# Issuing operand sums three products ahead, and holding two older products back, in a fused attention and squared-ReLU MLP kernel

## The chip, the cores and the metric

The kernel runs on one core of one Trainium2 chip. The metric is device time in microseconds (us). Unless said otherwise, a quoted time is the median over the timed runs of a kernel.

The names of the engines are those of the profile: PE is the tensor engine's matmuls, PEld its weight loads, DVE the vector engine, ACT the scalar engine, POOL the GpSimd engine, SP the engine that issues most DMAs.

## The reference

```python
# attention, per batch (8) and head (12), S = 448, D = 64
scores = (1/sqrt(D)) * q @ k.T
attn   = maximum(scores, 0)**2 / S
x      = attn @ v                       # regrouped to 3584 tokens x 768
# MLP, w_in 768 x 2048, w_out 2048 x 768
h = x @ w_in
g = maximum(h, 0)**2
out = g @ w_out
```

## The kernel before

Attention for batch b+1 is woven into the MLP of batch b. A queue (`fifo`) holds the MLP's pieces, and each turn of the attention loop takes a share of it.

- "scores" (tile sp) are turned into tile at, by ACT and DVE or by ACT and POOL.
- "h groups" are x @ w_in: six matmuls each, then ACT and DVE make a slice of g from them.
- The last product, g @ w_out, is done for two 128-token chunks at once in Strassen-like form: seven products m1 to m7 of 8 matmuls each instead of eight. It needs four sums of blocks of g, made by DVE (tile comb):

```python
def s1(): combine("s1", nc.vector.tensor_add, get2()[:, lo], get2()[:, hi])
def s2(): combine("s2", nc.vector.tensor_sub, st["s1"], get1()[:, lo])
def s3(): combine("s3", nc.vector.tensor_sub, get1()[:, lo], get2()[:, lo])
def s4(): combine("s4", nc.vector.tensor_sub, get1()[:, hi], st["s2"])
# order of the products:      m1   m2   m6   m5   m7   m3   m4
# sums that must be made:      0    0    2    2    3    4    4
```

m1 and m2 read g directly. m6 reads s2, m5 reads s1, m7 reads s3 and m3 reads s4. Most products end in a "part" (ACT) or a "close" (DVE, tile osb) that takes the result out of PSUM.

This is where a sum is issued. All sums of a batch wait in a queue; a product takes from it what it needs, at the moment when it is itself issued:

```python
def item(k=k, fn=fn, need=due + (0, 0, 2, 2, 3, 4, 4)[k]):
    nonlocal used
    while made < need:
        sum_one()
    fn()
    used += 2 <= k < 6
```

The attention loop also issues one sum each turn, ahead of the two at operations, as long as fewer than six are unused (there are six buffers). Where several products are issued in one turn of the loop, or where the loop is over (the last batch), no such sum has been made, and the product itself issues it.

The work for batch b is queued by `push_dense(b)`. Products left over from earlier batches (`old`, from `backlog`) are spread between the 16 h groups:

```python
for i, g in enumerate(hs):
    push([g])
    upto = (i + 1) * len(old) // len(hs)
    for z in old[done:upto]:
        push(z)
    done = upto
...                     # rest copies of odd batches (POOL), then the new sums become available
for z in backlog[:now]: # new products: m1, m2, m6, ...
    push(z)
```

"rest" is a copy by POOL that gathers the last 64 tokens of two batches into one chunk.

Of the kernel before, what the change touches and what calls it, by code (L numbers as in the profile page):

```python
# [16 lines left out]
def kernel(  # L17
# [123 lines left out]
    def combine_w2(k, eng):  # L141
        a, step = k % 2, k // 2
        top, bot, r = w2[a], w2[2 + a], slice(4 * a, 4 * a + 4)
        if step == 0:
            eng.tensor_sub(t1[:, r], top[:, :, HI], top[:, :, LO])
        elif step == 1:
            eng.tensor_sub(t2[:, r], bot[:, :, HI], t1[:, r])
        elif step == 2:
            eng.tensor_sub(t4[:, r], t2[:, r], bot[:, :, LO])
        else:  # L150
            eng.tensor_sub(top[:, :, HI], bot[:, :, HI], top[:, :, HI])  # L151
# [10 lines left out]
    def push(work):  # L162
        nonlocal queued
        for c, fn in work:
            fifo.append((c, fn))
            queued += c
# [3 lines left out]
    def run_some(ns):  # L170
        nonlocal queued, credit
        credit += ns
        while fifo and credit > 0:
            c, fn = fifo.popleft()
            fn()
            queued -= c
            credit -= c
# [12 lines left out]
    def h_groups(b):  # L190
        gt = gts[b] = g_p.tile([P, NF, S], FP16, name="g", tag="g")
        xt = xts[b]

        def group(f):
            def run():
                hps = mm_p.tile([P, 512], FP32, name="hps", tag="mm")
                for m in range(NM):
                    nc.tensor.matmul(  # L198
                        hps[:, 0:S],
                        lhsT=w1[f // 4][:, m, (f % 4) * P:(f % 4 + 1) * P],  # L200
                        rhs=xt[:, m, :], start=(m == 0), stop=(m == NM - 1))
                relu2(hps[:, 0:S], gt[:, f, :], 1.0)
            return run

        return [(189.0 * NM, group(f)) for f in range(NF)]
# [10 lines left out]
    def rest(pr):  # L216
        t = rest_p.tile([P, NF, P], FP16, name="rest", tag="rest")
        for i in range(2):
            nc.gpsimd.tensor_copy(  # L219
                t[:, :, 64 * i:64 * i + 64], gts[2 * pr + i][:, :, 3 * P:S])  # L220
        rests[pr] = t

    def chunk(b, c):
        return lambda: gts[b][:, :, c * P:(c + 1) * P], [(b, 2 * c), (b, 2 * c + 1)]

    def rest_chunk(pr):
        return lambda: rests[pr], [(2 * pr, TJ - 1), (2 * pr + 1, TJ - 1)]

    def plain_groups(one):
        get, at = one  # L230

        def group(cols):
            def run():
                ps = mm_p.tile([P, 512], FP32, name="ops", tag="mm")
                for f in range(NF):
                    nc.tensor.matmul(  # L236
                        ps[:, 0:HALF], lhsT=get()[:, f, :], rhs=w2[f // 4][:, f % 4, cols],
                        start=(f == 0), stop=(f == NF - 1))
                osb = part_p.tile([P, HALF], FP32, name="osb", tag="part")
                nc.scalar.activation(out=osb, in_=ps[:, 0:HALF], func=AF.Copy, scale=CO)  # L240
                store(at, cols, osb)
            return run

        return [(162.5 * NF, group(cols)) for cols in (LO, HI)]
# [75 lines left out]
    sums: deque = deque()  # L320
    made = used = due = 0

    def sum_one():
        nonlocal made
        sums.popleft()()
        made += 1

    def chain(pairs):

        nonlocal due  # L330
        new = []
        for _, groups in pairs:
            for k, (c, fn) in enumerate(groups):
                def item(k=k, fn=fn, need=due + (0, 0, 2, 2, 3, 4, 4)[k]):
                    nonlocal used
                    while made < need:
                        sum_one()
                    fn()
                    used += 2 <= k < 6
                new.append([(c, item)])  # L340
            due += 4
        return new, lambda: sums.extend(fn for four, _ in pairs for fn in four)
# [4 lines left out]
    def push_dense(b):  # L347

        hs = h_groups(b)
        ready = None  # L350
        if b == 0:
            new = [[g] for c in range(2) for g in plain_groups(chunk(b, c))]
        elif b % 2 == 0:
            new, ready = chain([o_groups(chunk(b, 0), chunk(b, 1))])
        else:
            pr = b // 2
            pairs = [o_groups(chunk(b - 1, 2), chunk(b, 0)), o_groups(chunk(b, 1), chunk(b, 2))]
            if pr % 2 == 1:
                pairs.insert(1, o_groups(rest_chunk(pr - 1), rest_chunk(pr)))
            new, ready = chain(pairs)  # L360
        old = backlog[:QUOTA[b]]
        done = 0
        for i, g in enumerate(hs):
            push([g])
            upto = (i + 1) * len(old) // len(hs)
            for z in old[done:upto]:
                push(z)
            done = upto
            if b == 0 and 4 <= i < 16 and i % 2 == 1:
                push([(0.0, lambda k=(i - 4) // 2: combine_w2(k, nc.gpsimd))])  # L370
        if b % 2 == 1:
            push([(0.0, lambda: rest(b // 2))])
        if ready:
            push([(0.0, ready)])
        backlog[:] = backlog[len(old):] + new
        now = QUOTA[b] - len(old)
        for z in backlog[:now]:
            push(z)
        del backlog[:now]
        if b == 0:  # L380
            push([(0.0, lambda k=k: combine_w2(k, nc.gpsimd)) for k in (6, 7)])
# [7 lines left out]
    def scores(n, t):  # L389
        qT, kT = qkt[n, "q"], qkt[n, "k"]  # L390
        sp = s_p.tile([P, 2, 512], FP32, name="sp", tag="s")
        for e in range(2):
            for f in range(2):
                c = f ^ e
                r = slice(64 * f, 64 * f + 64)
                nc.tensor.matmul(  # L396
                    sp[64 * c:64 * c + 64, e, 0:S].rearrange("p (t c) -> p t c", t=TJ),
                    lhsT=kT[r, t, 64 * e:64 * e + 64],
                    rhs=qT[r, :, 64 * e:64 * e + 64], start=True, stop=True)
        return sp  # L400

    def soft(n, t, sp, pool=False):
        at = at_p.tile([P, 2, S], FP16, name="at", tag="at")
        if pool:
            relu2_wide(sp[:, :, 0:S], at, SK, nc.gpsimd)
        elif n < NU and t % 2 == 1:
            relu2_wide(sp[:, :, 0:S], at, SK, nc.gpsimd if n == 1 and t == 3 else nc.vector)
        else:
            relu2(sp[:, :, 0:S], at, SK)
        ats[n, t] = at  # L410
# [42 lines left out]
    def av_burst(n):  # L453
        return (TJ * (n + 1) - 1) // 2 + 2
# [25 lines left out]
    with tc.manual_schedule():  # L480
# [19 lines left out]
        for w in "kq":  # L500
# [3 lines left out]
        beside = {  # L504
            1: [(load_w1, 1)],
            2: [(cast_qk, 2, "k", pool), (cast_qk, 2, "q", pool),
                (load_qk, 3, "k", nc.sync), (load_qk, 3, "q", nc.sync)],
            3: [(turn_pe, 1, "k", dve), (load_w1, 2)],
            5: [(turn_pe, 1, "q", act), (load_w1, 3)],
            7: [(turn_pe, 2, "k", dve)],  # L510
            8: [(turn_pe, 2, "q", act), (load_v, 3)],
            9: [(cast_qk, 3, "k", pool), (cast_qk, 3, "q", pool),
# [11 lines left out]
        for r in range(STREAM):  # L524
# [5 lines left out]
            for fn, *a in beside.get(r, ()):  # L530
                fn(*a)
    tc.no_sync_barrier()
    push_dense(0)

    for i in range(STREAM // 2, NB):
        g = []
        for r in range(max(STREAM, 2 * i), 2 * i + 2):
            n, t = divmod(r, TJ)
            g.append((n, t, scores(n, t)))
        if sums and made - used < 6:  # L540
            sum_one()
        for z, a in enumerate(g):
            soft(*a, pool=z == 1 and (i > av_burst(2 * NU - 1) or i % 2 == 1))
        if i in avs:
            for t in range(TJ):
                av(avs[i], t)
        if i in pushes:
            push_dense(pushes[i])
        upkeep(i)
        nxt = min([j for j in pushes if j > i] or [NB + 2])  # L550
        run_some(max(0.0, (queued - KEEP) / (nxt - i)))
# [4 lines left out]
    for j in sorted(j for j in pushes if j >= NB):  # L556
        push_dense(pushes[j])
# [31 lines left out]
```

## Time and profile before

| | before |
|---|---|
| time, median of 2 runs | 465.34 us (463.84 to 466.84) |
| span of the profiled run | 464.5 us |
| PE busy | 396.0 us, 85% |
| PE idle (span less busy) | 68.5 us |
| of it, waiting for sums | 47.4 us in 19 waits |
| mean granted tensor engine clock | 0.937 |

The page gives the busy time of each engine, with its share of the span and the number of instructions. Of the second part of the page, the two rows below show PE's busy share and the granted clock in 40 slices of 11.6 us, in tenths (9 is 90% or more).

```profile
PE 396.0 (85%) x3000; PEld 194.2 (42%) x3000; DVE 283.0 (61%) x363; ACT 250.1 (54%) x386; POOL 223.4 (48%) x191
PE   6769998999599996997798998989479997896864
PEclk9756999999889998999889999999789999999899
```

PE bounds the kernel. After the start (the first five slices) its holes have a pattern: slices of 4 to 7 busy, and in or just behind most of them slices of clock below 9.

The list of waits names who waited for whom, with total us, number of waits and the longest.

```profile
PE ops L272 <- DVE comb L253: 47.4, 19, 6.0
PE sp L396 <- ACT rel L187: 6.6, 7, 1.6
PE sp L396 <- DVE at L181: 5.7, 8, 1.6
```

So the sums account for 47.4 of the 68.5 idle us. The timeline of the tail (batch 7, when no attention is left) shows how one such wait comes about. Columns: start in us, duration, engine, line, operation, what is written and read, number of instructions, and in brackets the idle time before it and what ended it. Rows that do not matter are cut.

```profile
418.35 2.76 PE L272 MATMUL ops<-w,g 128*128 128x384 f16 x16
...
421.20 0.56 DVE L283 SCALAR_TENSOR_TENSOR osb<-ops,part 128x384 f32<-128x384 f32 x1 [1.46 <-PE ops L272]
421.68 0.68 DVE L253 TENSOR_TENSOR comb<-g 128x1024 f16<-128x1024 f16 x1
422.39 0.69 DVE L253 TENSOR_TENSOR comb<-comb,g 128x1024 f16<-128x1024 f16 x1
...
423.14 2.77 PE L272 MATMUL ops<-wt,comb 128*128 128x384 f16 x16 [2.03 <-DVE comb L253]
...
427.78 0.56 DVE L283 SCALAR_TENSOR_TENSOR osb<-ops,part 128x384 f32<-128x384 f32 x1 [4.09 <-ACT part L278]
428.25 0.68 DVE L253 TENSOR_TENSOR comb<-g,comb 128x1024 f16<-128x1024 f16 x1
...
428.99 1.47 PE L272 MATMUL ops<-w,comb 128*128 128x384 f16 x8 [1.77 <-DVE comb L253]
```

The inputs of s1 and s2 were complete when the last g was written at 419.74. DVE had nothing to do from then to 421.20. But the close of m2 stands ahead of the sums in DVE's queue, and it can start only when PE has finished m2. So PE finishes m2, DVE closes it, DVE makes s1 and s2, and only then can PE go on with m6: 2.03 us. The same happens with s4, behind the close of m7, which itself starts only when ACT's part of m7 is done (the bracket): 1.77 us.

Beside attention the waits are longer, because a sum also meets POOL. This is batch 5, from the timeline of the kernel before:

```profile
328.90 0.96 POOL L96 CAST qs<-qf 128x896 f16<-128x896 f32 x1
328.96 5.06 DVE L253 TENSOR_TENSOR comb<-comb,g 128x1024 f16<-128x1024 f16 x1
329.78 2.04 POOL L219 COPY rest<-g 128x1024 f16<-128x1024 f16 x2
331.77 1.69 POOL L188 TENSOR_TENSOR at<-rel 128x896 f16<-128x896 f32 x1
```

And from its timeline of PE alone, the product that waited for the sum:

```profile
334.07 4.46 PE L272 MATMUL ops<-wt,comb 128*128 128x384 f16 x16 [6.05 <-DVE comb L253]
```

A sum of 0.68 us lasts 5.06 us, to 0.56 us after the end of POOL's unbroken run at 333.46. That POOL's run holds the sum is my reading of these times. The last line also shows the second cost: 16 matmuls in 4.46 us behind the wait, which take 2.77 us elsewhere. The granted clock was 0.50 from 331.5 to 337 us; the texts below call this half-rate.

### The profile page before, as it was taken

What the parts mean: (1) busy time and instruction counts of PE and PEld (TensorE: products, weight loads), DVE (VectorE), ACT (ScalarE), POOL (GpSimd) and SP (SyncE); (2) the same over time, 40 slices, a digit from 0 to 9 for tenths busy, and PEclk for the clock granted to TensorE, in tenths of its full rate; (3) what the DMA queues carried; (4) which work ended last, traced back from release to release, by engine and by line L of the source; (5) the groups of instructions that cost most, each with busy time, mean ns of one, the idle gap of its engine ahead of it and who ended that gap; (6) DMA issues with size and microseconds to landing.
All of it is one profiled execution on the core that took longest, in us unless ns stands there. A gap on an engine that the chain in (4) does not pass through costs nothing.

```text
span 464.5 us, 7617 instructions
## 1 busy us (share of the span) xinstructions
PE 396.0 (85%) x3000; PEld 194.2 (42%) x3000; DVE 283.0 (61%) x363; ACT 250.1 (54%) x386; POOL 223.4 (48%) x191
## 2 busy tenths in 40 slices
PE   6769998999599996997798998989479997896864
PEld 2434444444244443443344454444235443453432
DVE  3886885466756764667657766656846663454341
ACT  3876786566337763676256664757145772242101
POOL 6553799697526762566444654653724332000000
PEclk9756999999889998999889999999789999999899
DMA  9999992746637364563627355454513011200222
GB/s 257 290 259 216 243 191 51 180 120 138 139 87 148 69 155 116 87 159 102 155 53 174 66 147 157 71 137 117 95 35 73 1 35 34 52 0 19 67 68 51
DMA packets 67618, 53.57 MB, mean 115 GB/s; under 512 B 36864, under 2 KB 67584, under 8 KB 67584
## 3 DMA queue, kind: packets, MB, share of 16 engines
q1 hardware_dynamic: 55152, 40.84, 33.8%
q0 software_dynamic: 12160, 11.80, 16.2%
q8 instruction: 23, 0.38, 0.4%
q10 hardware_dynamic: 272, 0.46, 0.3%
q14 instruction: 11, 0.09, 0.1%
HBM read 45.61 MB, written 11.01 MB: 122 GB/s over the span
## 4 chain that ended last, share of the span: by engine, by line
PE 69%; DVE 11%; ACT 8%; issue 5%; POOL 4%; DMA 1%; SPq 1%; ACTq 0%; DVEq 0%; POOLq 0%
PE hps L198 27%; PE ops L272 25%; PE sp L396 7%; PE avt L428 6%; DVE comb L253 5%; DVE at L181 3%; ACT at L180 3%; ACT rel L187 2%; ACT part L278 1%; DVE osb L283 1%; PE ops L236 1%; PE warm L495 1%; POOL w L151 1%; POOL at L188 1%; DMA qf<-in_q_dram 1%
## 5 line engine op out<-in xcount | busy, mean ns | idle before, releaser
L188 POOL TENSOR_TENSOR at<-rel 128x896 f16<-128x896 f32 x67 | 112.4, 1678 | 148.1 <-ACT rel L187 148.0
L198 PE MATMUL hps<-xt,w 128*128 128x448 f16 x768 | 157.4, 356 | 1.1 <-ACT xt L435 0.7
L181 DVE SCALAR_TENSOR_TENSOR at<-sp,at 128x896 f16<-128x896 f32 x93 | 100.5, 1089 | 49.8 <-ACT at L180 49.3
L181 DVE SCALAR_TENSOR_TENSOR g<-hps,g 128x448 f16<-128x448 f32 x128 | 79.1, 623 | 57.8 <-ACT g L180 57.7
L198 PEld LDWEIGHTS <-w 128*128 128x128 f16 x768 | 72.5, 98 | 78.0 <-issue 17.2
L180 ACT ACTIVATE g<-hps 128x448 f16<-128x448 f32 x128 | 70.0, 549 | 62.8 <-PE hps L198 62.8
L180 ACT ACTIVATE at<-sp 128x896 f16<-128x896 f32 x93 | 84.1, 915 | 32.5 <-PE sp L396 32.4
L272 PEld LDWEIGHTS <-comb 128*128 128x128 f16 x416 | 40.8, 104 | 88.0 <-DVE comb L253 55.3
L278 ACT ACTIVATE part<-ops 128x384 f32<-128x384 f32 x52 | 25.6, 493 | 89.9 <-PE ops L272 89.8
L187 ACT ACTIVATE rel<-sp 128x896 f32<-128x896 f32 x75 | 69.3, 924 | 5.1 <-POOL at L188 2.9
L272 PE MATMUL ops<-wt,comb 128*128 128x384 f16 x208 | 44.7, 376 | 28.1 <-DVE comb L253 28.1
L396 PE MATMUL sp<-qT,kT 64*64 64x448 f16 x672 | 56.0, 391 | 13.4 <-ACT rel L187 6.6
L283 DVE SCALAR_TENSOR_TENSOR osb<-ops,part 128x384 f32<-128x384 f32 x52 | 28.8, 555 | 57.4 <-PE ops L272 29.6
L272 PE MATMUL ops<-w,comb 128*128 128x384 f16 x208 | 38.5, 329 | 19.4 <-DVE comb L253 19.4
L428 PE MATMUL avt<-at,vs 64*64 64x448 f16 x672 | 44.8, 379 | 0.9 <-DVE g L181 0.6
L396 PEld LDWEIGHTS <-kT 64*64 64x64 f16 x672 | 16.8, 109 | 47.1 <-issue 44.5
L272 PEld LDWEIGHTS <-g 128*128 128x128 f16 x264 | 25.7, 100 | 21.5 <-issue 6.2
L121 POOL DMA_DIRECT2D vs<-in_v_dram x48 | 29.9, 631 | 9.2 <-DMA w<-in_moe_w_in_dram 9.1
L272 PE MATMUL ops<-w,g 128*128 128x384 f16 x176 | 30.9, 326 | 0.0
L428 PEld LDWEIGHTS <-vs 64*64 64x64 f16 x672 | 22.4, 114 | 13.3 <-issue 3.4
L219 POOL COPY rest<-g 128x1024 f16<-128x1024 f16 x8 | 8.1, 1040 | 33.8 <-DVE g L181 33.8
L253 DVE TENSOR_TENSOR comb<-g 128x1024 f16<-128x1024 f16 x22 | 22.2, 1009 | 0.0
(45 smaller groups left out, 232.4 us busy)
## 6 DMA issues: line engine op xcount, KB each, us to landing
out_dram<-osb SPq DMA_DIRECT2D x112, 96.0 KB, 2.2
kf<-in_k_dram SPq DMA_DIRECT2D x22, 448.0 KB, 4.5
qf<-in_q_dram SPq DMA_DIRECT2D x21, 448.0 KB, 5.3
vs<-in_v_dram POOLq DMA_DIRECT2D x48, 112.0 KB, 4.1
w<-in_moe_w_in_dram POOLq DMA_DIRECT2D x4, 768.0 KB, 20.3
w<-in_moe_w_out_dram POOLq DMA_DIRECT2D x4, 768.0 KB, 18.7
early<-in_k_dram SPq DMA_DIRECT2D x2, 448.0 KB, 7.4
early<-in_q_dram SPq DMA_DIRECT2D x2, 448.0 KB, 9.2
```

Of the source, the lines that this page charges most:

```text
L121: nc.gpsimd.dma_start(out=t[64 * r:64 * r + 64], in_=src[:, u, hs])
L180: nc.scalar.activation(out=dst, in_=ps, func=AF.Square, scale=scale)
L181: nc.vector.scalar_tensor_tensor(out=dst, in0=ps, scalar=0.0, in1=dst, op0=ALU.is_gt, op1=ALU.mult)
L187: nc.scalar.activation(out=r, in_=ps, func=AF.Relu, scale=scale)
L188: eng.tensor_mul(dst, r, r)
L198: nc.tensor.matmul(hps[:, 0:S], lhsT=w1[f // 4][:, m, (f % 4) * P:(f % 4 + 1) * P], rhs=xt[:, m, :], start=(m == 0), stop=(m == NM - 1))
L253: op(t, x, y)
L272: nc.tensor.matmul(st[bank][:, 0:HALF], lhsT=st[a][:, j, :], rhs=w(j), start=(first and j == 0), stop=(j == NH - 1), skip_group_check=True)
L278: nc.scalar.activation(out=st[name], in_=st[bank][:, 0:HALF], func=AF.Copy, scale=CO)
L283: nc.vector.scalar_tensor_tensor(out=osb, in0=st[bank][:, 0:HALF], scalar=sign * CO, in1=st[name], op0=ALU.mult, op1=ALU.add)
L396: nc.tensor.matmul(sp[64 * c:64 * c + 64, e, 0:S].rearrange("p (t c) -> p t c", t=TJ), lhsT=kT[r, t, 64 * e:64 * e + 64], rhs=qT[r, :, 64 ...
L428: nc.tensor.matmul(ap[f][64 * e:64 * e + 64, 0:S], lhsT=vs[r, e ^ c, t * D:(t + 1) * D], rhs=at[r, e, :], start=(t == 0), stop=(t == TJ - ...
```

## The change

Intent: a product asks for the sums of the product three places further on (never past the end of its own batch's list, and never with six sums unused), so that they are in DVE's queue ahead of the closes that wait for PE. And two of the older products are kept out of the h groups and put behind them, so that PE has work while DVE makes the first sums of the new batch.

```diff
+    AHEAD, SUMS = 3, 6
...
+        last = due + 4 * len(pairs)
+        needs = (0, 0, 2, 2, 3, 4, 4)
         for _, groups in pairs:
             for k, (c, fn) in enumerate(groups):
-                def item(k=k, fn=fn, need=due + (0, 0, 2, 2, 3, 4, 4)[k]):
+                z = k + AHEAD
+                def item(k=k, fn=fn, need=due + needs[k],
+                         want=min(last, due + needs[z % 7] + z // 7 * 4)):
                     nonlocal used
-                    while made < need:
+                    while made < need or (made < want and made - used < SUMS):
                         sum_one()
...
         old = backlog[:QUOTA[b]]
+        beside = max(0, len(old) - 2)
...
-            upto = (i + 1) * len(old) // len(hs)
+            upto = (i + 1) * beside // len(hs)
...
         if ready:
             push([(0.0, ready)])
+        for z in old[done:]:
+            push(z)
```

No matmul, sum or transfer is added or removed. Batches 1, 3 and 7 have no older products, so for them only the first part acts.

More of the change, by code (lines that the diff above doesn't have):

```diff
@@ L539 @@
             g.append((n, t, scores(n, t)))
-        if sums and made - used < 6:
+        if sums and made - used < SUMS:
             sum_one()
```

## The prediction

> **What bounds the kernel now.** TensorE. The page's busy table: PE 396.0 of 464.5 us (85%), DVE 283.0, ACT 250.1, POOL 223.4; the chain that ended last is 69% PE and 5.3% sums (DVE "comb", L253). PE's largest idle item in the list of waits is PE ops L272 <- DVE comb L253: 47.4 us in 19 waits, longest 6.0. The PE timeline places them: batch 1, 3.95+2.60; batch 2, 3.95+1.77; batch 3, 3.95+2.60+1.39; batch 4, 2.03; batch 5, 6.05+2.60; batch 6, 2.03+1.32+1.77; batch 7 (tail, no attention left), three times 2.03+1.77 = 11.4.
>
> Issue order makes them: a sum enters DVE's queue only when its product is next, behind the close of the product before (which waits for PE) and behind "at" (1.09 us). A free sum takes 0.68 us, but the 52 take 55.9 us instead of 35.4: some last 2.07, 3.08 and 5.06 us, until a run of POOL ops ends. [...]
>
> The waits also cost clock: after them 16 matmuls take 4.45 us instead of 2.77. I count 13 us (3.0, 1.7, 3.3, 3.4, 1.7 at 120, 177, 222, 334, 436). [...] the granted clock there is 0.7 to 0.8.
>
> **What changes.** No matmul, sum or byte is added. s1 and s2 are issued before m1 (2.6 us of PE work cover 1.4 us of sums), s3 before m2, s4 before m6. In batches 2, 4, 5 and 6 two older products go behind the h groups: 2.6 us more cover. Batch 5's s2 would start about 2 us earlier, before POOL's run of casts.
>
> **Sum.** Tail: waits (11.4) and clock (1.7) go nearly whole: 21 products x 1.30 = 27.3 us plus the last 4.5, so 46 becomes 32 to 33. Batches 1 to 6: of 36 us of waits about 30 go; in batches 1 and 3 the "rest" copies (2 x 1.03 us on POOL, right behind h) still block s1, about 1 us each, and other collisions leave some 4. Clock: 9 of the remaining 11. Returned: "at" stands behind up to four sums (2.7 us), so scores and attention products wait longer, and new waits on ACT and POOL appear: 5 us. Net 13 + 30 + 9 - 5 = 47, rounded to 45: 465 becomes 420 us. Nearly all is on the critical path: PE had work behind every one of these waits.
>
> **Predicted: 420 us**, 8 in 10 between 410 and 434. Faster by over 2%: 0.95; within 2%: 0.04; slower: 0.01.
>
> **Signs.** Right: PE <- comb falls from 47.4 to under 10 us, none in the tail; PE busy about 385 us, over 90% of the span; no half-rate matmuls behind h; mean granted clock from 0.937 to about 0.96; tail after the last h 32 to 33 us; scores' waits for "at" and "rel" rise from 12 to at most 18 us. Wrong: sums last 2 us and more beside POOL and the comb waits stay, or scores, attention or h wait as much as was saved.
>
> **What would make it wrong.** Earlier sums may meet POOL's ops head on and hold DVE's queue, delaying "at" and g; a sum waiting for one of six buffers would block DVE; the half-rate clock may come back elsewhere.

## The result and the profile after

The changed kernel takes 415.38 us (414.22 to 416.55, 2 runs) against 465.34 us. The ratio is 0.8926, 95% interval 0.8763 to 0.909. A ratio here is the mean time of one kernel's fast runs over that of the other's of the same rounds, so it is not quite the ratio of the medians. A second measurement of the same kernel (e5 below) gave 413.97 us and 0.895.

The page's busy times and slices of the changed kernel:

```profile
PE 382.4 (92%) x3000; PEld 191.9 (46%) x3000; DVE 282.3 (68%) x363; ACT 250.9 (61%) x386; POOL 225.4 (54%) x191
PE   6777999899989999999899999998969998999995
PEclk9855999999999999999999999999989999999998
```

Its list of waits (scores are L405 here, because lines were added):

```profile
PE sp L405 <- DVE at L181: 11.2, 10, 3.4
PE sp L405 <- ACT rel L187: 7.1, 8, 1.6
PE ops L272 <- ACT at L180: 1.6, 2, 0.8
...
PE ops L272 <- DVE comb L253: 0.9, 1, 0.9
```

The span fell by 464.5 - 414.7 = 49.8 us. It splits in two. PE's busy time fell by 396.0 - 382.4 = 13.6 us although the matmuls are the same 3000: that is clock (mean granted 0.963 instead of 0.937), and the row of granted clock is full almost everywhere behind the start. PE's idle time fell by 68.5 - 32.3 = 36.2 us: the waits for sums fell by 46.5 as the list names them, and scores' waits for at and rel grew by 18.3 - 12.3 = 6.0; other small waits took the rest, 4.3 us, of which 1.6 are waits for sums under another name.

That is a trap in reading: two waits of 0.81 us are put down to "ACT at L180". They are m6 behind h in batches 1 and 3, and the weight load of the same product names DVE comb. They are waits for s2. So 2.5 us of waits for sums are left, not 0.9, and these waits fell by 44.9 us.

The tail, from the timeline of the changed kernel:

```profile
381.16 2.76 PE L272 MATMUL ops<-w,g 128*128 128x384 f16 x16
...
381.94 0.62 DVE L181 SCALAR_TENSOR_TENSOR g<-hps,g 128x448 f16<-128x448 f32 x1 [0.51 <-ACT g L180]
382.60 0.69 DVE L253 TENSOR_TENSOR comb<-g 128x1024 f16<-128x1024 f16 x1
382.63 1.57 POOL L219 COPY rest<-g 128x1024 f16<-128x1024 f16 x1 [26.85 <-DVE g L181]
...
383.33 1.41 DVE L253 TENSOR_TENSOR comb<-comb,g 128x1024 f16<-128x1024 f16 x1
384.79 2.77 PE L272 MATMUL ops<-wt,comb 128*128 128x384 f16 x16 [0.86 <-DVE comb L253]
...
387.40 2.76 PE L272 MATMUL ops<-w,comb 128*128 128x384 f16 x16
```

s1 and s2 now follow directly on the last g. One wait of 0.86 us is left, because POOL's copy for rest and s2 hold each other up (s2 lasts 1.41 us instead of 0.69, the copy 1.57 instead of 1.04). The two further pairs have no wait at all, and from m1 to the end of the span the tail takes 414.7 - 381.2 = 33.5 us instead of 464.5 - 418.35 = 46.1.

The largest wait that is left is again in batch 5 (timeline of the changed kernel):

```profile
300.45 4.73 DVE L253 TENSOR_TENSOR comb<-g 128x1024 f16<-128x1024 f16 x1
301.15 0.96 POOL L96 CAST ks<-kf 128x896 f16<-128x896 f32 x1
302.02 0.96 POOL L96 CAST qs<-qf 128x896 f16<-128x896 f32 x1
302.92 1.70 POOL L188 TENSOR_TENSOR at<-rel 128x896 f16<-128x896 f32 x1
305.10 1.08 DVE L181 SCALAR_TENSOR_TENSOR at<-sp,at 128x896 f16<-128x896 f32 x1
306.23 0.59 PE L405 MATMUL sp<-qT,kT 64*64 64x448 f16 x4 [3.37 <-DVE at L181]
```

s3 is held for 4.73 us while POOL works without a break. It is not needed yet, but at stands behind it in DVE's queue, and scores wait for at: 3.37 us. Not every sum lasts until POOL's work ends: in batch 1 of the changed kernel a sum of 1.14 us ended while two rest copies were under way, which together took 2.48 us (2.01 in the kernel before). The sums did not get shorter: 52 of them take 54.9 us, and took 55.9. They only stand where fewer things wait for them.

### The profile page after: what moved, and what is told of

Its sections match the earlier page's. It is cut to its first block, busy times and chain, and to the rows that moved or that the text cites. A ratio compares the mean times of both kernels' runs of the same rounds, so it can differ in the third digit from the quotient of the medians.

```text
span 414.7 us, 7626 instructions
## 1 busy us (share of the span) xinstructions
PE 382.4 (92%) x3000; PEld 191.9 (46%) x3000; DVE 282.3 (68%) x363; ACT 250.9 (61%) x386; POOL 225.4 (54%) x191
## 3 DMA queue, kind: packets, MB, share of 16 engines
q0 software_dynamic: 12160, 11.80, 18.3%
## 4 chain that ended last, share of the span: by engine, by line
PE 72%; DVE 9%; ACT 8%; issue 5%; DMA 3%; POOL 2%; SPq 0%; ACTq 0%; DVEq 0%; POOLq 0%
PE hps L198 31%; PE ops L272 25%; PE sp L405 8%; PE avt L437 7%; DVE at L181 3%; ACT rel L187 3%; DVE comb L253 3%; ACT at L180 3%; DMA kf<-in_k_dram 2%; PE ops L236 1%; POOL w L151 1%; ACT g L180 1%; DVE g L181 1%; PE tps L110 1%; DVE osb L283 1%
## 5 line engine op out<-in xcount | busy, mean ns | idle before, releaser
L180 ACT ACTIVATE g<-hps 128x448 f16<-128x448 f32 x128 | 70.1, 550 | 55.5 <-PE hps L198 55.5
L180 ACT ACTIVATE at<-sp 128x896 f16<-128x896 f32 x93 | 84.1, 915 | 24.6 <-PE sp L405 24.5
L405 PE MATMUL sp<-qT,kT 64*64 64x448 f16 x672 | 55.3, 382 | 19.3 <-DVE at L181 11.2
L272 PEld LDWEIGHTS <-comb 128*128 128x128 f16 x416 | 39.6, 99 | 34.5 <-issue 6.1
L405 PEld LDWEIGHTS <-kT 64*64 64x64 f16 x672 | 16.9, 108 | 53.1 <-issue 50.1
L272 PE MATMUL ops<-wt,comb 128*128 128x384 f16 x208 | 37.9, 334 | 2.5 <-ACT at L180 1.6
L272 PE MATMUL ops<-w,comb 128*128 128x384 f16 x208 | 36.5, 326 | 0.0
L253 DVE TENSOR_TENSOR comb<-g 128x1024 f16<-128x1024 f16 x22 | 25.6, 1163 | 0.1
L219 POOL COPY rest<-g 128x1024 f16<-128x1024 f16 x8 | 10.1, 1275 | 28.0 <-DVE g L181 28.0
```

The costliest lines, as they stand in the source:

```text
L180: nc.scalar.activation(out=dst, in_=ps, func=AF.Square, scale=scale)
L253: op(t, x, y)
L272: nc.tensor.matmul(st[bank][:, 0:HALF], lhsT=st[a][:, j, :], rhs=w(j), start=(first and j == 0), stop=(j == NH - 1), skip_group_check=True)
L405: nc.tensor.matmul(sp[64 * c:64 * c + 64, e, 0:S].rearrange("p (t c) -> p t c", t=TJ), lhsT=kT[r, t, 64 * e:64 * e + 64], rhs=qT[r, :, 64 ...
```

## The experiments

Theory: the order of issue makes the waits, and the lookahead takes them away; the two kept products matter little. Rivals: the kept products do the work; or the sums, or POOL's interference, became shorter; or the clock is no separate cost. Columns of this summary: time, ratio to the kernel before with its interval, then from the profile PE's waits for sums, scores' waits for at, DVE time of all sums (us), and mean granted clock. PE's waits are those under the name "DVE comb"; in the changed kernel, e1, e2, e3, e5, e10, e11 and e12 two more of 0.8 us stand under "ACT at L180".

| run | time | ratio (95%) | PE <- comb | sp <- at | sums on DVE | clock |
|---|---|---|---|---|---|---|
| before | 465.34 | 1 | 47.4 | 5.7 | 55.9 | 0.937 |
| changed kernel | 415.38 | 0.8926 (0.8763 to 0.909) | 0.9 | 11.2 | 54.9 | 0.963 |
| e1 lookahead alone | 418.47 | 0.9013 (0.8969 to 0.9057) | 8.2 | 7.7 | 55.6 | 0.957 |
| e2 kept products alone | 449.69 | 0.9684 (0.9626 to 0.9742) | 33.2 | 5.8 | 53.5 | 0.951 |
| e3 lookahead 1 | 410.36 | 0.8841 (0.8797 to 0.8884) | 2.2 | 8.0 | 52.2 | 0.988 |
| e4 before, waits filled | 452.49 | 0.9754 (0.9712 to 0.9795) | 13.2 | 5.5 | 55.5 | 0.977 |
| e5 changed kernel again | 413.97 | 0.895 (0.8912 to 0.8987) | 0.9 | 12.3 | 54.9 | 0.982 |
| e6 before, sums twice | 507.69 | 1.0981 (1.0942 to 1.1021) | 73.4 | 11.5 | 96.6 | 0.921 |
| e7 changed, sums twice | 446.99 | 0.9657 (0.9586 to 0.9728) | 14.0 | 19.6 | 97.7 | 0.95 |
| e8 lookahead 1, rest later | 422.25 | 0.911 (0.9066 to 0.9154) | 5.2 | 10.7 | 60.5 | 0.965 |
| e9 lookahead 1, rest on ACT | 409.42 | 0.8827 (0.88 to 0.8854) | 2.9 | 5.8 | 52.8 | 0.979 |
| e10 lookahead 1, at first | 433.08 | 0.9334 (0.9303 to 0.9365) | 15.5 | 5.7 | 76.5 | 0.967 |
| e11 lookahead 6 | 420.72 | 0.9067 (0.9036 to 0.9099) | 0.9 | 16.0 | 57.1 | 0.969 |
| e12 lookahead 2 | 419.25 | 0.9059 (0.9033 to 0.9085) | 0.9 | 13.1 | 60.0 | 0.972 |

All results were correct. Runs e1 to e4, e5 to e8, e9 to e11 and e12: the kernel before took 463.65, 462.69, 463.77 and 463.48 us in them. The clock at the very start differs from run to run (mean granted clock of the first 60 us: 0.77 in the profile of the kernel before, 0.80 in that of the changed one), and so does the time that follows: the first product of batch 1 starts at 112.31 us in the profile of the kernel before, at 111.74 in the changed one and at 108.59 in e3. So spans of single profiles carry about 3 us of chance, and the times decide.

### e1: the lookahead alone

```diff
-        beside = max(0, len(old) - 2)
+        beside = len(old)
```

> The change without its second part: sums three products ahead, but no older products kept behind h. Theory (issue order makes the waits, the lookahead removes them): the tail and batches 1, 3 and 7, which had nothing to keep, are as in the changed kernel; batches 2, 4, 5 and 6 lose 2.6 us of cover each, so 1 to 5 us of PE waits come back: 416 to 421 us, PE waits for sums under 6 us. Rival (the two kept products give PE the work that hides the sums): most of the gain goes, 440 us or more.

From its list of waits, and from its timeline of DVE:

```profile
PE ops L272 <- DVE comb L253: 8.2, 5, 6.0
```

```profile
300.95 6.57 DVE L253 TENSOR_TENSOR comb<-comb,g 128x1024 f16<-128x1024 f16 x1
```

418.47 us, as expected. The 45.2 us to the kernel before (463.65) are nearly the whole gain. Of the 8.2 us of waits that remain (expected: under 6), 6.05 are one wait, again s2 of batch 5, which lasted 6.57 us, presumably beside POOL as in the kernel before. The kept products are worth about 3 us by the ratios (0.9013 against 0.8926 and 0.895), near the edge of what the intervals can tell.

### e2: the kept products alone

```diff
-    AHEAD, SUMS = 3, 6
+    AHEAD, SUMS = 0, 6
```

> The other part alone: lookahead 0, two older products kept behind each h. Theory: the tail keeps its 11.4 us of waits and batches 1 and 3 theirs; only the first wait of batches 2, 4, 5 and 6 shrinks, by at most 2.6 us each (and their clock loss, some 3 us): 452 to 462 us, PE waits for sums 35 to 43 us. Rival (kept products matter most): 430 us or less.

From its list of waits:

```profile
PE ops L272 <- DVE comb L253: 33.2, 16, 4.0
```

449.69 us: 14.0 us faster than before, somewhat more than expected (its waits for sums, 34.8 us with the two under another name, are also just below the 35 to 43 us expected), and far from the rival's 430. The first waits of batches 2, 4, 5 and 6 shrink to at most 1.31 us (in batch 2, for instance, 3.95 becomes 0.81); the tail keeps its 11.4. Alone the parts give 45 and 14 us, together 49 to 50: they hide some of the same waits. The kept products have a small cost as well: h and the attention products wait 3.9 us for ACT and DVE here and in the changed kernel, against 1.7 us in e1 and in the kernel before.

### e3, e5, e11, e12: how far ahead

```diff
-    AHEAD, SUMS = 3, 6
+    AHEAD, SUMS = 1, 6        # e3;  2 in e12;  6 in e11;  e5 is the changed kernel unedited
```

> Lookahead of one product instead of three, two products kept. Theory: what counts is that a sum is ahead of the close that waits for PE; in the tail s1 and s2 are then issued before m2, behind the close of the pair before, and are ready 2.1 us after m1 starts, while m1 and m2 take 2.6 us: no wait in the tail but the one behind the rest copies. Beside attention 1.3 us less cover gives 1 to 6 us: 416 to 422 us. Rival (all three products of lead are needed): waits of about 1 us per pair and more come back, 428 us or more.

> The changed kernel itself, unedited, beside the three others of this call, so that they can be compared on one chip: 413 to 418 us. Against it the lookahead of one (e3) can be put: theory that a lookahead of three costs time, because sums then stand ahead of the at operation in DVE's queue, has this 3 to 6 us slower than the 410.4 us of e3; rival that e3 was a lucky draw has both at about the same ratio to the kernel before, 0.884.

> Lookahead of six products, two kept. Theory (what a sum needs is to be ahead of its product by about 2 us; more only puts more sums ahead of at): all four sums of a pair stand ahead of the next at, scores' waits for at rise from 12 to 14 to 18 us, none of the waits for sums is left beside attention that a lookahead of three has not removed: 415 to 421 us. Rival (deeper is better or the same): 414 us or less.

> Lookahead of two, two products kept: the point between e3 (one, ratio 0.884) and the changed kernel (three, ratios 0.893 and 0.895). Theory (s1 and s2 gain nothing beyond one product of lead, and each further product puts s3 and s4 ahead of one more at): s3 comes before m6 and s4 before m5, scores' waits for at between 8 and 12 us, 409 to 415 us, ratio 0.882 to 0.895. Rival (single collisions with POOL's runs decide, not the order against at): outside 405 to 418 us on either side.

A lookahead of one gives 410.36 us, faster than I expected and faster than the change itself (413.97 and 415.38; the interval of its ratio ends at 0.8884, that of e5 begins at 0.8912). One product of lead is enough to come ahead of the close. A lookahead of six gives 420.72 us, as expected: no wait for sums is left that three had not removed, and scores' waits for at rise to 16.0 us. In batch 5 the sums ahead of at cost this much with six (PE's timeline of e11), against 3.37 us with three:

```profile
310.49 0.59 PE L405 MATMUL sp<-qT,kT 64*64 64x448 f16 x4 [4.57 <-DVE at L181]
```

With a lookahead of one that wait is gone there; m7 and m3 wait 0.78 and 0.61 us instead.

But the series is not even: one, two, three and six give ratios of 0.884, 0.906, 0.895 and 0.907. Lookahead two lies outside what I expected of the theory and on the rival's side. Its profile shows a wait of 2.51 us for at in batch 1, where three has 1.05, and its sums take 60.0 us on DVE, so they were held more than with three (54.9), presumably by POOL. That profile was also the fastest of its five runs (416.66 us), so it does not show the whole difference; this stays open. What the series supports is: one is enough, more is no gain, and the exact figure depends on which sum meets which run of POOL.

### e4: the waits of the kernel before, filled with matmuls

```diff
+        def spare(bank, n):          # into a bank that the next product overwrites
+            st[bank] = mm_p.tile([P, 512], FP32, name="ops", tag="mm")
+            for j in range(n):
+                nc.tensor.matmul(st[bank][:, 0:HALF], lhsT=st["a11"][:, j % NH, :],
+                    rhs=w2_block(0, j % NH, LO), start=True, stop=True, ...)
         def m6():
+            if fill[0]: spare("z", fill[0])
...
         def m3():
+            if fill[1]: spare("w", fill[1])
...
+    FILL = {1: (20, 12), 2: (20, 8), 3: (20, 12), 4: (8, 0), 5: (30, 12), 6: (8, 8), 7: (9, 8)}
```

> The kernel before, with matmuls that nobody needs put into the waits for sums (9 to 30 of 0.163 us, each fewer than the wait it stands in, into a bank that the next product overwrites). The issue order of the sums is unchanged. Theory (13 us of the 465 are half-rate clock that follows the idle time): the half-rate matmuls behind the waits go, the waits themselves stay: 450 to 456 us, mean granted clock 0.96. Rival (clock is no cost of its own, the time is all waiting): 465 us, or more by what the fillers add.

452.49 us, 11.2 us less than the kernel before beside it, with 209 matmuls more (8 to 30 in each wait; the expectation says 9). From its list of waits:

```profile
PE ops L272 <- DVE comb L253: 13.2, 19, 1.4
```

And from its timeline, the first wait of batch 1 (L300 are the fillers):

```profile
113.57 3.42 PE L300 MATMUL ops<-w,g 128*128 128x384 f16 x20
...
117.59 2.77 PE L272 MATMUL ops<-wt,comb 128*128 128x384 f16 x16 [0.60 <-DVE comb L253]
```

The waits themselves are unchanged in sum: 209 fillers of 0.163 us are 34.1 us, and with the 13.2 us that stayed idle that makes 47.3, as before. But the 16 matmuls behind this wait take 2.77 us, not 4.21 as in the kernel before. From 110 to 130 us the mean granted clock is 1.00 here and was 0.90 there, from 325 to 345 us 1.00 and 0.81. So some 11 us of the 465 were clock lost to the idle times, apart from the idle times themselves. In the kernel before, four of the five slow sets of 16 matmuls (4.21 to 4.46 us) stand behind waits of 3.95 to 6.05 us, but the fifth (4.45 us) stands behind one of the three waits of 2.03 us in the tail. The fillers went into the long and the short waits together.

### e6 and e7: every sum twice

```diff
             op(t, x, y)
+            op(t, x, y)
             st[name] = t
```

> The kernel before with every sum issued twice into the same buffer (52 more of at least 0.68 us on DVE; results stay right). Theory: in the kernel before, sums stand on the critical path, one or two of them in each of 19 waits; the tail alone gains 3 x (1.4 + 0.7) = 6 us, the others 10 to 20 us with what they meet of POOL: 480 to 495 us. Rival (sums were not on the path, the waits are for something else): under 470 us.

> The changed kernel with every sum issued twice. Theory: sums are as long as before but off the critical path, so the same 35 us and more of added DVE time costs under half of what it costs in the kernel before: 1.4 us in the tail's first pair, the rest where at stands behind the sums: 417 to 427 us. Rival (sums are still on the path, only shorter waits): +20 us and more, 435 us or above.

Both cost more than expected. DVE's time for sums grew by 40.7 us in the kernel before (96.6 - 55.9) and by 42.8 us in the changed one (97.7 - 54.9). The kernel before lost 507.69 - 462.69 = 45.0 us, the changed one 446.99 - 413.97 = 33.0 us. So "under half", which I had written, is refuted: the changed kernel still pays three quarters of what the kernel before pays (33.0 of 45.0 us), and the rival's "435 us or above" holds. The list of waits of e7:

```profile
PE sp L406 <- DVE at L181: 19.6, 12, 4.8
PE ops L273 <- DVE comb L254: 14.0, 7, 4.0
```

The lookahead hides the sums at their present length and has little slack. m1 and m2 cover 2.6 us; s1 and s2 take 1.4 us, and twice that when doubled: in the tail's first pair PE waits 2.31 us. Only the two later pairs of the tail behave as the theory said: their sums are issued a product earlier still, and even doubled they make PE wait nowhere.

### e8 and e9: the rest copies

```diff
 e8 (lookahead 1): the copies are queued behind the first two new products
-        if b % 2 == 1:
-            push([(0.0, lambda: rest(b // 2))])
...
-        for z in backlog[:now]:
+        for j, z in enumerate(backlog[:now]):
             push(z)
+            if j == 1 and b % 2 == 1:
+                push([(0.0, lambda: rest(b // 2))])

 e9 (lookahead 1): ACT makes the copies, in their old place
-            nc.gpsimd.tensor_copy(
+            nc.scalar.copy(
```

> Lookahead of one, two products kept, and the copies of rest moved behind the first two products of the new pair, so that they no longer stand on POOL when s1 and s2 start. Theory (the 0.8 to 0.9 us waits left in batches 1, 3 and 7 are s1 held by POOL's read of rest): these three waits go, 2.5 us, 406 to 409 us. Rival (they come from the last g and the sum's own time): no change, 410 us.

> Lookahead of one, two products kept, and the rest copies done by ACT instead of POOL, in their old place. Theory (the three waits of 0.8 to 0.9 us left behind h are s1 held while POOL reads for rest): these waits fall to 0.2 us or less and POOL's runs get 2 us shorter in every odd batch, while ACT, 62% busy, takes 8 copies of about 1 us: 405 to 409 us, ratio to the kernel before 0.875 to 0.882. Rival (these waits are the sums' own time behind the last g): the waits stay, and ACT's 8 us delay at and part: 410 us or more.

e8 is a miss: 12 us slower than e3. The 0.81 us waits of batches 1 and 3 did go, but that of the tail stayed at 0.86 (POOL has nothing else to do there, so the copy still started right on the last g, at 387.58, wherever it was queued), scores in batches 1 and 3 now wait 2.45 us for at, and in batch 5 the moved copies joined a run of POOL that was already long (timeline of DVE in e8):

```profile
306.21 6.58 DVE L253 TENSOR_TENSOR comb<-g 128x1024 f16<-128x1024 f16 x1
```

And the product that waited, from the timeline of PE in e8:

```profile
312.85 4.08 PE L272 MATMUL ops<-w,comb 128*128 128x384 f16 x16 [4.36 <-DVE comb L253]
```

e9 takes the copies away from POOL altogether, and is the direct test of who held s1. Batch 1, from its timeline:

```profile
109.86 1.98 ACT L219 COPY rest<-g 128x1024 f16<-128x1024 f16 x2
...
110.65 0.69 DVE L253 TENSOR_TENSOR comb<-g 128x1024 f16<-128x1024 f16 x1
111.38 0.69 DVE L253 TENSOR_TENSOR comb<-comb,g 128x1024 f16<-128x1024 f16 x1
...
112.41 2.77 PE L272 MATMUL ops<-wt,comb 128*128 128x384 f16 x16
```

With the copies on ACT, s1 and s2 take their free 0.69 us and m6 waits no more; in the tail the wait falls from 0.86 to 0.30 us, and the trace puts what is left down to ACT, whose part of m1 now stands behind the copies. So POOL's copies were the cause; "POOL's read" in the expectations stands for them, and no run tells their reading from their writing. The total, 409.42 us, is just outside what I expected and level with e3: in batch 5 m7 now waits 2.90 us for another sum, which presumably meets POOL. e3 and e9 are the fastest kernels.

### e10: at ahead of the loop's sum

```diff
-        if sums and made - used < SUMS:
-            sum_one()
         for z, a in enumerate(g):
             soft(*a, ...)
+        if sums and made - used < SUMS:
+            sum_one()
```

> Lookahead of one, two products kept, and in the attention loop the one sum of each turn issued behind the at operations instead of ahead of them. Theory (a sum ahead of at delays it, and scores wait): scores' waits for at fall from 8 to 6 us, but a sum then comes up to 1.1 us later for its product: 408 to 411 us. Rival (POOL's runs alone decide): a change of either sign of over 4 us, from other collisions with POOL.

433.08 us, 23 us slower than e3: the expectation was far off, and the rival's wording (POOL decides) fits. Scores' waits for at fell as expected, from 8.0 to 5.7 us. But the sums take 76.5 us on DVE instead of 52.2, and the waits for them rise to 15.5. s3 of batch 1 in the timeline of e10:

```profile
115.73 1.68 POOL L188 TENSOR_TENSOR at<-rel 128x896 f16<-128x896 f32 x1 [1.46 <-ACT rel L187]
116.20 1.75 DVE L253 TENSOR_TENSOR comb<-g 128x1024 f16<-128x1024 f16 x1
```

In e3 the same sum began ahead of POOL's at (113.00 against 113.52) and took 0.68 us. There the sum, ahead of at, was nearly done while POOL still waited for ACT's rel (1.46 us, until 113.52); behind at, it meets POOL's half of the same turn (115.73 to 117.41).

## Why the prediction was right

The predicted 420 us (410 to 434) against 415.38 us: the direction, the size and the place of the gain were right. The size owes something to luck, because terms that were off cancel. From the two profiles: waits for sums 44.9 us less (predicted 11.4 + 30 = 41.4), clock 13.6 (10.7), given back 8.7 (5), together 49.8 us of span; predicted were 47, rounded down to 45.

- **Waits for sums.** Predicted under 10 us, measured 0.9 plus the two of 0.81 that carry another name. I had left about 6 us in batches 1 to 6; of 36 us there 34.4 went. This term and the clock's were larger than predicted, and what was given back took most of the difference away again.
- **Cause by issue order.** e1 shows that the lookahead alone brings nearly all, and e2 that the kept products do not. That the sums still take 54.9 us shows that they became no cheaper.
- **Clock.** Predicted 1.7 + 9 = 10.7 us, measured 13.6 us as PE's busy time (the 0.7 to 0.8 that the prediction names can be read from the slices of 11.6 us; over the 4.5 us right behind the five waits the granted clock is 0.62 to 0.67). e4 shows separately that about 11 us of clock can be had back without touching the order of the sums. "No half-rate matmuls behind h" was nearly right: 8 matmuls behind the 3.37 us wait of batch 5 took 2.71 us instead of 1.47 (granted clock 0.50 from 306.2 to 309 us).
- **Tail.** Predicted 32 to 33 us, measured 33.5. "None in the tail" was wrong by one wait of 0.86 us: I had counted the rest copies against s1 in batches 1 and 3 and forgotten the one in batch 7. e9 shows that it was this copy.
- **Batches 1 and 3.** About 1 us each was predicted to stay because of the rest copies: 0.81 us each stayed, and e9 shows the cause.
- **Batch 5.** s2 did start before the casts, as predicted, and took 1.61 us. Its place in POOL's run was taken by s3, which I had not seen.
- **What is given back.** Predicted 5 us, measured 44.9 - 36.2 = 8.7: this term was undersized. Scores' waits for at and rel grew by 6.0 us, to 18.3 ("at most 18"), and 2.2 us are the waits of h and the attention products that came with the kept products (e2). e3 suggests that part of the 6.0 belonged to the depth of three: one product of lead has 8.0 us of waits for at instead of 11.2 and is 4 to 5 us faster; but with two (e12) these waits are 13.1 us, so depth is not all.

What the prediction did not see is that a smaller lookahead would do better, and how thin the slack is: my own expectations for e7, e8 and e10 took the sums to be safely off PE's path, and each was wrong: in e8 and e10 because sums then stand beside another POOL instruction (one of 6.58 us in e8; in e10 s3 of batch 1 took 1.75 us instead of 0.68), in e7 because doubled sums are longer than what covers them.

## What to carry to other kernels

Look at what stands ahead of a small operation in its engine's queue. Here DVE was idle from 419.74 to 421.20 us with a sum's inputs complete and then did the close first; 0.7 us operations, one or two at a time, cost waits of 1.3 to 6 us, because they were issued behind operations that waited for the very engine they were to feed. Issue them just early enough to be ahead of that wait; more lead puts them in front of something else (here at: scores' waits for it were 8.0 us with a lead of one and 16.0 with six). And after moving them, read their durations again on the trace, because a second engine that holds them up, as POOL does here (5.06, 4.73 and 6.58 us for a sum of 0.68 in the kernel before, the changed one and e8), may decide more than the order does.
